# A two-headed state-space kernel on one core: one broadcast load, one first-stage step, one down product and one evacuation change places in a hand-kept order

## The chip, the core and the metric

The kernel runs on one core of a Trainium2 chip. The metric is the time of one execution in device microseconds. TensorE (PE in the profile) multiplies, VectorE (DVE), ScalarE (ACT) and GpSimd (POOL) do the rest, and SyncE (SP) issues nearly all DMAs.

## The reference

Two independent heads, D = 640 channels each, 2048 time steps, bf16 in and out; their outputs stand side by side in the last axis.

```
# head A: diagonal complex state space, P = 640 states
dt = exp(log_dt);  Lam_bar = exp(dt * Lam)
B_bar = ((Lam_bar - 1) / Lam)[:, None] * Bmat
Bu = einsum("bld,pd->blp", x, B_bar)
h[t] = Lam_bar * h[t-1] + Bu[t]            # 2048 steps
y = 2 * Re(einsum("blp,dp->bld", h, Cmat)) + x * Dskip
# head B: gated long convolution
k_shift[t] = sum over j < 4 of k[t-j] * shift_k[j]
kv = k_shift * v
y = irfft(rfft(pad(kv)) * rfft(pad(ssm_k)))[:2048] + kv * ssm_D
out = q * y
```

## The kernel before

Everything lives in one SBUF tile, `arena`, cut into named parts, and one PSUM tile, `acc`, used as eight banks of 512 f32 columns. `build` records 815 operations with their footprints; `depend` derives who must wait for whom. The table `ORDER` then says in which order they are issued, on which engine, and in which bank. An entry `666A6` is operation 666, on ACT (`A`; `V` is DVE, `T` PE, `G` POOL, `S` SP), first bank 6. A small `t` is PE with the product cut into two halves of 64 weight columns ("narrow"), a capital `T` is the full 128-column form, where the operation has both. Each engine executes its own entries strictly in the table's order, and each waits for its operands and for the last reader of its bank. SP is such an engine too: an issue that waits holds back every issue behind it.

Head A turns the recurrence into a tree of 16 time classes. `up2`, `up1` and `up0` multiply x by the scaled B and combine pairs (L581, L602); `coarse` scans 128 blocks (`cs_...`, L679 and the lines near it); `down(n, js)` goes back down the tree in levels 3 to 0: the product `dn` on PE (L229 narrow, L225 full), then the add `ad` on DVE (L728). `project(i)` makes one sixteenth of the output rows: `ld_r` loads x (L736), `xd` multiplies it by D's row (L737), `C` is the product with C (L229 or L225), `ev_C` adds the two (L754), `st_A` stores (L765). D's row is `Dskip` repeated over 128 partitions, 160 KB, loaded once by `ld_Dr` (operation 91, L372); every `xd` reads it, `xd0` first.

Head B does the convolution by Fourier stages as products. `load_h` brings the filter (`ld_h`, L807) and adds `ssm_D` to its first tap (`addD`, L809). `load_kv` brings k and v by transposing DMAs (L814), `conv` makes kv (taps L205 on DVE or L206 on ACT, adds L840, product L841), `plane` writes kv to DRAM (`pl`, L847), and `relay` reads it back in another layout (`rl`, L857). Stage `s1` (L876 full, L881 narrow) is evacuated by `e1` (L886), stage `s2` (L900) by `e2` (L913); the product with the filter is `pp`, `pq`, `py`, `pz` (L924 to L931); `r2` (L951) and `r1` (L972) go back, and `er1`/`em1` multiply by q. Names carry half and unit: `s1h0_5` is first stage, filter, half 0, unit 5; `e2k1_27` evacuates the second stage of kv, half 1, planes 27 to 29.

The operations that the change touches, with their places in the order before:

- `ld_Dr` (91, SP): behind the four `ld_h1` loads of the second half's filter, ahead of `ld_r2`.
- `s1h0_5` (199, PE): behind `up0a_2`, in bank 0; its evacuation `e1h0_5` (200, ACT): behind `e1h0_2` and a small `cf`.
- `dn2_5` (344, PE): narrow, between `dn1_2` and `gC2_1`; its add `ad2_5` follows on DVE.
- `e2k1_27` (666): on ACT, between the evacuations `e2k1_14` and `e2k1_22`.

Of the kernel before, what the change touches and what calls it, by code (L numbers as in the profile page):

```python
# [1097 lines left out]
def plain_order(P):  # L1098
# [16 lines left out]


ORDER = (
# [40 lines left out]
)  # L1158


# [68 lines left out]
```

## Time and profile before

| what | value |
|---|---|
| three runs | 187.65, 188.11, 189.12 us; median 188.11 |
| span of the profiled execution, first to last instruction | 187.3 us |
| PE, DVE, ACT, POOL busy | 175.6, 158.0, 147.7, 72.6 us |
| granted TensorE clock | 0.999 |
| moved by DMA | 30.15 MB, mean 161 GB/s |

The profiler lists no separate time outside its own span for that execution, so the span stands 0.8 us under the median of the runs. A row of the timeline gives the start in microseconds, the duration, the engine, the line and the operation, how many follow each other, and in brackets the idle time of the engine before it with what ended it. A row of the chain gives start, duration and what held the end up then. Engine names with a q are sequencers: an SPq row's duration is the time that SP spent on the issue, not the transfer.

### The profile page before, as it was taken

What the parts mean: (1) busy time and instruction counts of PE and PEld (TensorE: products, weight loads), DVE (VectorE), ACT (ScalarE), POOL (GpSimd) and SP (SyncE); (2) the same over time, 40 slices, a digit from 0 to 9 for tenths busy, and PEclk for the clock granted to TensorE, in tenths of its full rate; (3) what the DMA queues carried; (4) which work ended last, traced back from release to release, by engine and by line L of the source; (5) the groups of instructions that cost most, each with busy time, mean ns of one, the idle gap of its engine ahead of it and who ended that gap; (6) DMA issues with size and microseconds to landing.
All of it is one profiled execution on the core that took longest, in us unless ns stands there. A gap on an engine that the chain in (4) does not pass through costs nothing.

```text
span 187.3 us, 7665 instructions
## 1 busy us (share of the span) xinstructions
PE 175.6 (94%) x3398; PEld 126.3 (67%) x3399; DVE 158.0 (84%) x225; ACT 147.7 (79%) x181; POOL 72.6 (39%) x68
## 2 busy tenths in 40 slices
PE   7998999999799979979997999999999999999992
PEld 2565666677468756656685688776588876887770
DVE  3537964679959899999969999899999999998961
ACT  2469699989899979999997997997898883985000
POOL 8679999900000000008803925730740000551620
PEclk9999999999999999999999999999999999999999
DMA  5999999799999989999989479402496993058996
GB/s 153 191 184 158 200 143 140 141 174 182 198 253 154 290 179 152 180 182 154 138 109 251 154 170 133 75 5 72 122 196 120 210 227 85 15 160 187 208 219 173
DMA packets 106682, 30.15 MB, mean 161 GB/s; under 512 B 101274, under 2 KB 106010, under 8 KB 106650
## 3 DMA queue, kind: packets, MB, share of 16 engines
q1 hardware_dynamic: 106332, 29.35, 86.7%
q8 instruction: 26, 0.43, 1.1%
q10 hardware_dynamic: 318, 0.33, 0.6%
q14 instruction: 6, 0.05, 0.1%
HBM read 11.32 MB, written 7.86 MB: 102 GB/s over the span
## 4 chain that ended last, share of the span: by engine, by line
PE 54%; DVE 23%; DMA 9%; ACT 8%; issue 3%; DVEq 0%; ACTq 0%
PE acc L225 17%; PE acc L581 13%; DMA arena<-in_B_k_dram 9%; PE acc L229 6%; DVE arena L728 6%; PE acc L900 6%; DVE arena L205 5%; ACT arena L913 5%; PE acc L951 4%; DVE arena L840 3%; PE acc L972 3%; PE acc L539 2%; DVE arena L754 2%; PE acc L881 1%; ACT arena L886 1%
## 5 line engine op out<-in xcount | busy, mean ns | idle before, releaser
L581 PE MATMUL acc<-arena 128*64 128x512 bf16 x400 | 45.6, 380 | 1.8 <-DVE arena L457 1.1
L913 ACT CAST arena<-acc 128x960 bf16<-128x960 f32 (+1 forms) x43 | 37.4, 916 | 4.0 <-PE acc L900 2.2
L225 PE MATMUL acc<-arena 128*128 128x320 bf16 (+2 forms) x255 | 36.4, 297 | 2.2 <-DVE arena L754 1.1
L581 PEld LDWEIGHTS <-arena 128*64 128x64 bf16 x400 | 26.0, 110 | 17.8 <-DVE arena L457 1.3
L886 ACT CAST arena<-acc 128x1024 bf16<-128x1024 f32 x37 | 35.8, 1034 | 2.1 <-PE acc L881 2.0
L225 PEld LDWEIGHTS <-arena 128*128 128x128 bf16 x256 | 23.7, 98 | 12.1 <-DVE arena L754 1.3
L841 POOL TENSOR_TENSOR arena<-arena 128x2048 bf16<-128x2048 bf16 x2 | 8.8, 4410 | 53.7 <-DVE arena L840 46.1
L900 PE MATMUL acc<-arena 128*64 128x160 bf16 x512 | 23.6, 235 | 1.8 <-DVE arena L679 1.4
L900 PEld LDWEIGHTS <-arena 128*64 128x64 bf16 x512 | 18.6, 110 | 8.3 <-ACT arena L913 2.2
L229 PE MATMUL acc<-arena 128*64 128x320 bf16 (+3 forms) x258 | 23.2, 313 | 0.5 <-DVE arena L690 0.5
L840 DVE TENSOR_TENSOR arena<-arena 128x2048 bf16<-128x2048 bf16 x14 | 17.6, 1256 | 4.5 <-ACT arena L206 4.3
L728 DVE TENSOR_TENSOR arena<-acc,arena 128x1024 bf16<-128x1024 f32 (+2 forms) x19 | 20.4, 1114 | 0.9 <-PE acc L229 0.5
L760 POOL TENSOR_TENSOR arena<-arena 128x640 bf16<-128x640 f32 x3 | 4.2, 1416 | 32.6 <-ACT arena L752 32.6
L956 ACT CAST arena<-acc 128x1024 bf16<-128x1024 f32 x16 | 15.4, 1025 | 1.7 <-PE acc L951 1.6
L229 PEld LDWEIGHTS <-arena 128*64 128x64 bf16 x258 | 13.0, 110 | 3.5 <-DVE arena L690 0.6
L876 PE MATMUL acc<-arena 128*64 128x128 bf16 x400 | 14.6, 220 | 0.2 <-ACT arena L886 0.2
L876 PEld LDWEIGHTS <-arena 128*64 128x64 bf16 x400 | 12.9, 110 | 2.4 <-ACT arena L886 0.9
L205 DVE TENSOR_SCALAR arena<-arena 128x2048 bf16<-128x2048 bf16 x15 | 11.0, 749 | 3.6 <-DMA arena<-in_B_k_dram 3.5
L754 DVE TENSOR_TENSOR arena<-acc,arena 128x640 bf16<-128x640 f32 x13 | 10.7, 820 | 3.5 <-PE acc L225 2.2
L206 ACT ACTIVATE arena<-arena 128x2048 bf16<-128x2048 bf16 (+2 forms) x10 | 11.1, 1112 | 1.5 <-DMA arena<-in_B_k_dram 1.5
L924 DVE TENSOR_TENSOR arena<-arena 128x2560 bf16<-128x2560 bf16 x8 | 11.9, 1484 | 0.1
L602 PE MATMUL acc<-arena 128*64 128x256 bf16 (+2 forms) x140 | 11.6, 291 | 0.1
(142 smaller groups left out, 284.4 us busy)
## 6 DMA issues: line engine op xcount, KB each, us to landing
out_dram<-arena SPq DMA_DIRECT2D x32, 160.0 KB, 3.3
arena<-in_B_ssm_k_dram SPq DMA_DIRECT2D x8, 320.0 KB, 6.1
kv_rows<-arena SPq DMA_DIRECT2D x5, 512.0 KB, 4.7
arena<-kv_rows SPq DMA_DIRECT2D x16, 160.0 KB, 4.0
arena<-in_A_x_dram SPq DMA_DIRECT2D x16, 160.0 KB, 3.5
arena<-in_B_q_dram SPq DMA_DIRECT2D x8, 320.0 KB, 6.3
arena<-in_A_B_im_dram ACTq DMA_DIRECT2D x1, 160.0 KB, 2.8
arena<-in_A_B_re_dram SPq DMA_DIRECT2D x1, 160.0 KB, 3.0
```

Source lines behind the costliest of these rows:

```text
L205: vm = lambda e: lambda out, in_, by: e.tensor_scalar_mul(out=out, in0=in_, scalar1=by)
L225: e.matmul(out, lhsT=lhsT, rhs=rhs, start=start, stop=stop, skip_group_check=True)
L229: e.matmul(out[half], lhsT=lhsT[:, half], rhs=rhs, start=start, stop=stop, skip_group_check=True, tile_position=(0, 64 * r))
L581: e.matmul(o[64 * r:64 * r + 64], lhsT=self.BT[j][:, r, d, :], rhs=self.XP[:, d, 2 * q:2 * q + 2], start=(d == 0), stop=(d == 4), skip_gro ...
L728: e.tensor_tensor(out=o, in0=b, in1=o, op=ALU.add)
L754: e.tensor_tensor(out=two(ys), in0=two(B)[:, :, 0:320], in1=two(ys), op=ALU.add)
L840: P.add(f"ca{d}_{j}", tt, lambda e: e.tensor_tensor(out=t1, in0=t1, in1=t2, op=ALU.add), outs=[t1], ins=[t1, t2])
L876: e.matmul(B[64 * b:64 * b + 64, 128 * i:128 * i + 128], lhsT=lh[i], rhs=F[:, b, :], start=True, stop=True, tile_position=(0, 64 * b))
L886: P.add(f"e1{what}{hf}_{u}", {PACT: act(1024), PDVE: dve(1024)}, lambda e, B: c.CP[e](out=out, in_=(B.rearrange("p (l n s k) -> p k s l n" ...
L900: e.matmul(B[64 * s:64 * s + 64, 512 * b + 160 * i:512 * b + 160 * i + 160], lhsT=c.W[:, k, 64 * b:64 * b + 64], rhs=self.AS[hf][:, k, 160 ...
L913: c.CP[e](out=out, in_=b.rearrange("p r (k j n) -> p r k j n", k=n, j=4) if nj > 1 else b.rearrange("p r (k x) -> p r k x", k=n))
L956: P.add(f"er2{hf}_{u}", {PACT: act(1024), PDVE: dve(1024)}, lambda e, B: c.CP[e](out=out, in_=B.rearrange("p (s n b) -> p b s n", s=2, n=4 ...
```

## The change

Only the table `ORDER` changes. Its lines are cut anew, so nearly all of them differ as text; as operations, these differ:

```diff
-    "204A0 401S0 140A0 190A4 398V0 199T0 193t2 16A0 138A0 231T4 403V0 194A2 137V0 24V0 402V0 271S0 142A0 200A0 404V0 80A0 197T0 "
+    "386V0 78G0 75A0 262V6 238A0 389S0 79G0 225T2 188V0 254A4 150G0 57A0 201T4 84G0 199T0 200A0 154A0 176S0 195T6 387V0 245T0 196A6 "
...
-    "458V0 439S0 344t4 457V0 351A6 283T0 501T2 345V4 459G0 284A0 348t6 502A2 91S0 466T0 349V6 352t4 467A0 291T2 353V4 470T6 "
+    "442S0 458V0 344T4 351A6 457V0 283T0 501T2 345V4 284A0 459G0 348t6 439S0 502A2 466T0 349V6 352t4 467A0 291T2 353V4 292A2 470T6 "
+    "411S0 301T4 256A6 320V0 410S0 313T0 302A4 316V0 318t2 257T6 447V0 314A0 91S0 415S0 309T4 446V0 258A6 158S0 310A4 319V2 448V0 "
...
-    "641T0 363V6 364t4 753G0 642A0 645T2 365V4 665T6 646A2 376t0 498G0 754S0 666A6 656T2 761S0 377V0 630T4 674S0 657A2 360t6 "
+    "498G0 376t0 754S0 761S0 666V6 377V0 656T2 674S0 630T4 657A2 360t6 675S0 361V6 631A4 632T2 756G0 370t0 633A2 634T4 371V0 652T6 "
```

1. `ld_Dr` is issued ahead of 18 other transfers of SP.
2. `s1h0_5` goes from behind `up0a_2` to between `s1h0_6` and `s1h0_3`, ahead of `s1h0_3`, `up1_4`, `s1h0_1`, `up1_0`, `up21_4`, `s1h0_7`, `s1h0_0` and `up0a_2`; `e1h0_5` goes ahead on ACT from behind `cf` to ahead of `cos`. Both keep bank 0.
3. `dn2_5` is made in the full form: four products of 128 weight columns instead of eight of 64.
4. `e2k1_27` is done by DVE, between the adds `ad0_3` and `ad0_9`, instead of by ACT.

The remaining swaps in the table (`em1` entries on POOL, which issue nothing where DVE did the multiplication, and entries of different engines) leave every engine's instructions as they were.

On SP, at the relay of the first half and at the filter loads of the second (L857 relay, L847 `pl2`, L795 `ld_D`, L736 `ld_r1` and `ld_r2`, L807 `ld_h1`):

```order
 L857 DMA arena<-kv_rows 32x40x64
 L847 DMA kv_rows<-arena 128x2048
+L372 DMA arena<-in_A_Dskip_dram 128x640
 L857 DMA arena<-kv_rows 32x40x64
 L795 DMA arena<-in_B_ssm_D_dram 4x80
...
 L736 DMA arena<-in_A_x_dram 128x640
 L807 DMA arena<-in_B_ssm_k_dram 32x80x64 x4
-L372 DMA arena<-in_A_Dskip_dram 128x640
 L736 DMA arena<-in_A_x_dram 128x640
 L814 DMA_TRANSPOSE arena<-in_B_v_dram 128x2048
```

D's row now stands behind the store `pl2` and ahead of the second relay read; `ld_r2` follows the filter loads directly.

On ACT, in the first stages (L622 `ev_up1_2` and `ev_up1_6`, L314 a table of sines, L478 `cos`, L886 the first-stage evacuations, the upper one of which is `e1h0_5` now and the lower one `e1h0_3`):

```order
 L622 CAST arena<-acc 128x2x2x256 x2
 L314 ACTIVATE arena<-arena 128x1024
+L886 CAST arena<-acc 128x64x2x8
 L478 ACTIVATE arena<-arena 128x1280
 L886 CAST arena<-acc 128x64x2x8
```

One evacuation more stands ahead of `cos`; the same one is missing later, ahead of a table of L354.

On DVE, in the last level of the tree and the second half's second stage (L728 the adds `ad0_2`, `ad0_3`, `ad0_9`, `ad0_1`, `ad0_6`; L913 `e2k1_27`; L924 `pp1`):

```order
 L929 TENSOR_TENSOR arena<-arena 128x8x4x40
 L927 TENSOR_TENSOR arena<-arena 128x8x160
-L728 TENSOR_TENSOR arena<-acc,arena 128x4x256 x5
+L728 TENSOR_TENSOR arena<-acc,arena 128x4x256 x2
+L913 CAST arena<-acc 128x2x3x160
+L728 TENSOR_TENSOR arena<-acc,arena 128x4x256 x3
 L924 TENSOR_TENSOR arena<-arena 128x2560
 L737 TENSOR_TENSOR arena<-arena 128x640
```

The run of five adds is split by one evacuation.

71 rows, old and new, of the table ORDER are left out of this document.

## The prediction

> **What bounds the kernel now.** I first read the page's span, then the busy times of the last part by window, then the chain of waits around the four places that the change touches.
>
> ```profile
> span 187.3 us, 7665 instructions
> 139.00:184.50 45.50, 44.38 (x1064) 34.89 (x1060) 41.01 (x50) 25.84 (x29) 9.79 (x6) 1.00 0.77 162
> ```
>
> The second row is a window: its length, then the busy time of PE, PE's weight loads, DVE, ACT and POOL, the granted clock, the share of the DMA engines and GB/s. From 139 us to the last engine work PE is busy for 44.38 of 45.50 us. So what comes late or early at 139 us comes late or early at the end; nothing in between is left to absorb it.
>
> Before that, who bounds changes by stage. The chain of waits, in two windows (start, duration, what ran or was waited for):
>
> ```profile
> 59.81 5.37 DMA arena<-in_B_k_dram
> ...
> 65.20 1.42 DVE arena L205 x2
> ```
>
> ```profile
> 133.34 1.19 DVE arena L728
> 134.61 1.22 DVE arena L728
> 135.91 1.24 DVE arena L728
> 137.19 1.93 PE acc L900 x48
> ```
>
> From 60 to 67 us the chain is made of a k transfer and what DVE does behind it; PE isn't in it. From 133 to 139 us it goes through three of DVE's five adds, each released by a product and itself releasing a bank, into the products that follow. An instruction given to DVE there is on the path.
>
> Between the two lies the one wait that names D's row:
>
> ```profile
> 95.96 0.53 DVE L809 TENSOR_TENSOR arena<-arena 128x80 bf16<-128x80 bf16 x1
> 97.87 0.49 DVE L737 TENSOR_TENSOR arena<-arena 128x640 bf16<-128x640 bf16 x1 [1.38 <-DMA arena<-in_A_Dskip_dram]
> 98.49 0.82 DVE L754 TENSOR_TENSOR arena<-acc,arena 128x640 bf16<-128x640 f32 x1
> 99.63 1.22 DVE L840 TENSOR_TENSOR arena<-arena 128x2048 bf16<-128x2048 bf16 x1
> 100.77 1.48 DVE L924 TENSOR_TENSOR arena<-arena 128x2560 bf16<-128x2560 bf16 x1
> 102.30 0.82 DVE L754 TENSOR_TENSOR arena<-acc,arena 128x640 bf16<-128x640 f32 x1
> ```
>
> ```profile
> 97.40 1.00 PE L881 MATMUL acc<-arena 64*64 64x64 bf16 x96
> 99.37 2.89 PE L225 MATMUL acc<-arena 128*128 128x320 bf16 x20 [0.97 <-DVE arena L754]
> ```
>
> DVE stands for 1.38 us until the row has landed, then makes `xd0` and `ev_C0`; PE stands for 0.97 us because `C1` needs the bank that `ev_C0` empties.
>
> **Part 1, D's row.** It is gone from its old place. `xd0` can start when `addD1` ends (95.96 + 0.53 = 96.49) and ends near 96.98. `C0`, ahead of the L881 products of 97.40 on PE, ends at about 97.5, so `ev_C0` starts at 97.5 instead of 98.49 and ends at 98.3; `C1` starts when the L881 products leave PE, 98.4 instead of 99.37: 1.0 us. DVE keeps less of it, since the add `ca4_0` (L840, 99.63) needs a tap of ACT:
>
> ```profile
> 96.80 2.04 ACT L206 ACTIVATE arena<-arena 128x2048 bf16<-128x2048 bf16 x1
> ```
>
> The tap ends at 98.84, so the add starts at 98.87, 0.76 earlier, the L924 product ends at 101.48 and `ev_C1` starts at 101.5 instead of 102.30. **0.8 us** stays. I take it to be kept until 133 us, since what follows on PE, DVE and ACT is released by each other's work, which all starts earlier; where it isn't, the last rival holds.
>
> Now the price at the new place, on SP and on the DMA engines:
>
> ```profile
> 64.26 0.42 SPq L857 DMA_DIRECT2D arena<-kv_rows  x1
> 64.74 1.61 SPq L795 DMA_DIRECT2D arena<-in_B_ssm_D_dram  x1
> 67.63 3.23 SPq L857 DMA_DIRECT2D arena<-kv_rows  x4
> 72.74 1.86 SPq L857 DMA_DIRECT2D arena<-kv_rows  x2
> 88.90 1.64 SPq L807 DMA_DIRECT2D arena<-in_B_ssm_k_dram  x1
> 90.58 3.45 SPq L372 DMA_DIRECT2D arena<-in_A_Dskip_dram  x1
> ```
>
> ```profile
> 68.00:95.00 27.00, 25.16 (x586) 17.80 (x583) 26.69 (x35) 26.25 (x33) 8.14 (x2) 1.00 1.08 151
> DMA to landing us min/median/max: 4.8/6.1/7.8
> arena<-kv_rows SPq DMA_DIRECT2D x16, 160.0 KB, 4.0
> ```
>
> The first row is the window from 68 to 95 us; the other two are the times from issue to landing of L807 and, as median, of the relay. An issue of 160 KB takes SP 0.42 us where it needn't queue, and SP's standing from 66.35 (64.74 + 1.61) to 67.63, where it waits for `pl2`, takes that up. The transfer itself isn't free: the DMA engines are full from 68 to 95 us, and 160 KB at 151 GB/s is 1.06 us by which everything behind comes later. Who notices? The last relay read, issued near 73.4, lands near 77.4, then 78.5; its reader starts at 78.65, and PE stands behind it:
>
> ```profile
> 78.65 0.64 PE L876 MATMUL acc<-arena 128*64 128x128 bf16 x16
> 80.09 0.22 PE L225 MATMUL acc<-arena 128*128 128x128 bf16 x1 [0.81 <-ACT arena L886]
> ```
>
> That is 0.15 us of slack and 0.81 us of standing. The last filter load, issued at 88.90, lands near 95.0, at the latest at 95.96, when `addD1` reads it without a wait. With 1.06 more it lands between 96.1 and 97.0; `xd0`, behind it on DVE, then ends between 97.1 and 98.0, and `ev_C0` starts between 97.5 and 98.0. So part 1 gives **−0.8 to −0.4 us**. I take −0.7, nearer to the median landing. The bound on the bad side is the issue's old length, 3.45 us, met again at the new place: that is the second rival, +0.2 us for this part.
>
> **Part 2, the evacuation on DVE.** By form:
>
> ```profile
> L913 ACT CAST arena<-acc 128x960 bf16<-128x960 f32 x33 | 31.1, 978 | 2.0 <-ACT arena L913 0.9 <-PE acc L900 0.3 <-DVE arena L737 0.3
> L913 DVE CAST arena<-acc 128x960 bf16<-128x960 f32 x3 | 3.5, 1154 | 0.0
> ```
>
> ACT loses 0.98 us and DVE gains 1.15 us, between the adds that end at 134.53 (133.34 + 1.19) and start at 134.61. In the chain the adds' steps are 1.30 us for 1.22 to 1.24 us of work: they stand 0.07 to 0.08 us before each for a product. Behind the evacuation the next two products are ready, so these two waits vanish and the cost is 1.15 − 0.15 − 0.08 (instructions of DVE overlap by as much: 100.77 lies before 99.63 + 1.22) = **0.92 us**. The third add of the chain, `ad0_1`, then ends at 138.1 instead of 137.15, the L900 products behind its bank start 0.9 later, and so does `C7` (at 139.12, 137.19 + 1.93), which opens the stretch in which PE is full. ACT has spare time of its own only where PE feeds it late, so its 0.98 us buys nothing. The bounds: 0 if the adds aren't what PE waits for, 1.15 if no wait vanishes; below zero if ACT set the pace there, by its 0.98 us:
>
> ```profile
> 132.71 8.79 ACT L913 CAST arena<-acc 128x960 bf16<-128x960 f32 x11 [0.34 <-PE acc L900]
> ```
>
> ACT runs eleven evacuations without a pause in 8.79 us. I take **+0.9**, since the chain names DVE.
>
> **Part 3, the first-stage step.** It brings a new wait: `up1_4`, behind it on PE, uses bank 0 too.
>
> ```profile
> 37.21 1.09 PE L876 MATMUL acc<-arena 128*64 128x128 bf16 x32
> 38.10 2.35 PE L581 MATMUL acc<-arena 128*64 128x512 bf16 x20
> 40.92 1.01 ACT L622 CAST arena<-acc 128x1024 bf16<-128x1024 f32 x1 [0.62 <-PE acc L602]
> 51.79 1.01 ACT L886 CAST arena<-acc 128x1024 bf16<-128x1024 f32 x1 [0.85 <-PE acc L881]
> 48.12 1.05 PE L581 MATMUL acc<-arena 128*64 128x512 bf16 x8 [1.15 <-DVE arena L457]
> 67.41 0.61 PE L900 MATMUL acc<-arena 128*64 128x160 bf16 x12 [1.39 <-DVE arena L679]
> ```
>
> The first row is `s1h0_6` and `s1h0_3`; `s1h0_5` takes the second's place and ends at 38.3 (37.21 + 1.09). ACT has its evacuation ahead of `cos` now, so it stands until then, and gives the bank free near 39.35 (1.01 us). `up1_4` starts near 39.4 instead of 38.10: 1.3 us late, and queued behind it on PE are `s1h0_1`, `up1_0`, `up21_4`, `s1h0_7`, `s1h0_0` and `up0a_2`. ACT, which begins `cos` only after 39.3, is 2 us late; it gets back its pauses of 0.62 and 0.85 us and the 1.0 us of the evacuation that it no longer makes at 53 us. PE stands 1.15 us before 48.12 for DVE's table, so `up0a_2` is late by 0.2 to 0.4 us, and 1.39 us before 67.41 for DVE, which is behind the k transfer of the chain above. Both engines wait there for something that part 3 doesn't touch. Cost **0** with that cover; up to 1.3 us without it.
>
> **Part 4, the full form of `dn2_5`.**
>
> ```profile
> 87.62 1.49 PE L229 MATMUL acc<-arena 128*64 128x512 bf16 x16
> 89.54 3.48 DVE L728 TENSOR_TENSOR arena<-acc,arena 128x1024 bf16<-128x1024 f32 x3
> ```
>
> Its last product ends at 89.11 and its add starts at 89.54, when DVE comes to it: 0.43 us of slack. The row's 16 products take 1.49 us, eight of them narrow ones of `dn2_5` and these the shorter ones, so the step as a whole is under 0.75 us and a change of its form by 0.43 us isn't to be expected. Cost 0, between −0.1 and +0.1 us. The Trainium skill, TensorEngine Tiling, Key Properties, says that a change of tiling mode drains TensorE, which speaks against one full-width step between `dn1_2`, narrow, and `gC2_1`. By that rule the step's start waits for `dn1_2` to leave the array; the row allows 0.43 us for it, so by the rule too the sum stays unless the drain is longer than that, and no row here times one by itself.
>
> **The sum** is made on the profiled span: 187.3 − 0.7 + 0.9 + 0 + 0 = 187.5 us. The median of the runs stands 0.8 us above the span; with that, **188.3 us**, as good as no change.
>
> **The rivals.**
>
> - *The gain stays, the evacuation is hidden.* ACT's eleven evacuations in a row are the limit from 132 to 141 us, so DVE's time is covered. For it: ACT shows no pause in that stretch. Against it: the chain goes through L728. 188.1 − 0.7 = 187.4 us.
> - *D's row holds up the filter (slower).* SP spends 3.45 us on the issue at 64.7 as it did at 90.58. Of these, 1.28 us vanish in SP's standing until 67.63; 2.2 us reach the filter loads, whose last lands between 97.2 and 98.2. `addD1` and `xd0` follow on DVE, `ev_C0` ends between 99.0 and 100.0 (at 99.31 now), so part 1 turns into −0.3 to +0.7, say +0.2, and part 2 stays. It decides once the last filter load lands later than about 97.4. For it: full DMA engines. Against it: the neighbours' issues of 0.42 us at that very place. 188.1 + 0.2 + 0.9 = 189.2 us.
> - *The first stage doesn't recover.* The 1.3 us at `up1_4` reaches 67 us. For it: ACT and PE are both busy there. Against it: 2.5 us of standing PE in between, and a chain that runs through DMA and DVE. 188.3 + 1.3 = 189.6 us.
> - *The gain doesn't arrive.* Something else ends DVE's wait at the same time, or a later stage is set by something that doesn't start earlier, such as the last v block behind `ld_Dr` on SP and the relay behind that. Then only part 2 is left: 188.1 + 0.9 = 189.0 us. Against it: the wait's own row names D's row, and the last v block, too, is freed of the 1.06 us ahead of it.
>
> **How the numbers follow.** The forecast has a chance of 0.62, the hidden evacuation 0.17, the late filter 0.10, the first stage 0.03, the last 0.05; 0.03 is left for what I don't see. All named cases lie between 187.4 and 189.6 us. With the runs' own spread around them, I take 187.2 to 189.3 us. A measurement of this kernel tells about 1% (1.9 us) from no change. Below 186.2 us none of the cases lies, and above 190.0 us only the first stage together with a late filter; so faster 0.03, same 0.93, slower 0.04.
>
> **What would show it.** Right: no DVE wait that names D's row; `C1` starts within 0.1 us of the L881 products' end; the adds at 133 to 138 us take one evacuation between them, and `C7` starts later relative to `C1` by 0.9 us. PE stands up to 0.9 us near 39 us and ACT 1 us ahead of it, its wait at 48 us nearly vanishes, the rest of the first stage is as before by 67 us. Wrong: a wait of `addD1` for the filter; a wait at L881 near 97 us; a distance from `C1` to `C7` as before (then the evacuation was hidden); a span below 186.5 or above 188.7 us.

## The result and the profile after

The changed kernel takes 189.05 us (median of 19 runs, 188.08 to 190.07), the kernel before 187.79 us on the same chip (19 runs, 187.17 to 191.13). The ratio is 1.0052, interval 1.0033 to 1.0071: 0.98 us slower, 0.62 to 1.33. It is estimated from the runs within 1.5% of the fastest of their kernel, which leaves out one of 191.13 us here and three in the experiment "Row at 29 us" below, and it isn't the quotient of the two medians, which stand 1.26 us apart. The change is under 1%, and the time lies inside the range of 187.2 to 189.3 us; the forecast was 188.3 us, +0.2.

The profiled execution of the changed kernel, its span and its last part by window:

```profile
span 187.9 us, 7657 instructions
139.00:184.50 45.50, 45.10 (x1088) 35.82 (x1082) 41.26 (x51) 26.57 (x30) 9.80 (x6) 1.00 0.76 161
```

This execution took 189.73 us, 1.8 us more than its span, and that distance is the same in the executions profiled later (187.49 for a span of 185.7). By it the profiled execution of before, 187.3 us of span, took 189.1 us: it was the slowest of the three runs shown.

DVE, SP and PE where D's row was awaited:

```profile
94.49 1.23 DVE L840 TENSOR_TENSOR arena<-arena 128x2048 bf16<-128x2048 bf16 x1
97.75 0.53 DVE L809 TENSOR_TENSOR arena<-arena 128x80 bf16<-128x80 bf16 x1 [2.03 <-DMA arena<-in_B_ssm_k_dram]
97.96 0.63 DVE L737 TENSOR_TENSOR arena<-arena 128x640 bf16<-128x640 bf16 x1
98.72 0.82 DVE L754 TENSOR_TENSOR arena<-acc,arena 128x640 bf16<-128x640 f32 x1
```

```profile
63.01 0.42 SPq L372 DMA_DIRECT2D arena<-in_A_Dskip_dram  x1
63.48 1.17 SPq L857 DMA_DIRECT2D arena<-kv_rows  x1
66.15 4.71 SPq L857 DMA_DIRECT2D arena<-kv_rows  x4
78.20 3.80 SPq L814 DMA_TRANSPOSE arena<-in_B_k_dram  x1
84.12 8.74 SPq L807 DMA_DIRECT2D arena<-in_B_ssm_k_dram  x4
```

```profile
98.37 1.00 PE L881 MATMUL acc<-arena 64*64 64x64 bf16 x96 [1.21 <-DVE arena L809]
99.60 2.89 PE L225 MATMUL acc<-arena 128*128 128x320 bf16 x20 [0.23 <-DVE arena L754]
```

The wait for D's row is gone, and a longer one, 2.03 us, stands one instruction earlier: `addD1` waits for the filter. The row's own issue took 0.42 us, as predicted. What grew are the issues behind it: the four relay reads 4.71 us (3.23 before), `ld_k4` 3.80 (2.16 before), the four filter loads 8.74 (7.61 before).

DVE at the five adds, of the kernel before and of the changed one:

```profile
132.18 6.09 DVE L728 TENSOR_TENSOR arena<-acc,arena 128x1024 bf16<-128x1024 f32 x5
138.18 1.48 DVE L924 TENSOR_TENSOR arena<-arena 128x2560 bf16<-128x2560 bf16 x1
```

```profile
132.36 2.36 DVE L728 TENSOR_TENSOR arena<-acc,arena 128x1024 bf16<-128x1024 f32 x2
134.63 1.15 DVE L913 CAST arena<-acc 128x960 bf16<-128x960 f32 x1
135.69 3.48 DVE L728 TENSOR_TENSOR arena<-acc,arena 128x1024 bf16<-128x1024 f32 x3
139.09 1.48 DVE L924 TENSOR_TENSOR arena<-arena 128x2560 bf16<-128x2560 bf16 x1
```

From the first add to the product behind the last, 6.00 us have become 6.73. PE, which had no wait of over 0.15 us in this stretch before, now waits for DVE twice, in the changed kernel:

```profile
135.83 0.62 PE L229 MATMUL acc<-arena 128*64 128x512 bf16 x4 [0.46 <-DVE arena L913]
138.09 1.85 PE L900 MATMUL acc<-arena 128*64 128x160 bf16 x48 [0.23 <-DVE arena L728]
```

The product `C7` starts 40.18 us behind `C1`, which was 39.59: 0.6 us of the 0.73 reach PE.

PE in the first stages:

```profile
37.60 1.53 PE L876 MATMUL acc<-arena 128*64 128x128 bf16 x48
39.84 2.35 PE L581 MATMUL acc<-arena 128*64 128x512 bf16 x20 [0.71 <-ACT arena L886]
42.83 0.64 PE L876 MATMUL acc<-arena 128*64 128x128 bf16 x16 [0.21 <-ACT arena L598]
...
52.71 2.35 PE L581 MATMUL acc<-arena 128*64 128x512 bf16 x20 [0.63 <-ACT arena L886]
...
67.47 1.22 PE L900 MATMUL acc<-arena 128*64 128x160 bf16 x24
...
71.21 0.61 PE L900 MATMUL acc<-arena 128*64 128x160 bf16 x12
```

`up1_4` waits 0.71 us for the new evacuation, and at 52.71 us PE stands again for ACT, 0.63 us, where it had no wait before. In this pair of profiles that seems to cost nothing: PE's waits at 48.12 and 67.41 us are gone and `s2h0_18` starts at 71.21 us, which was 71.54.

So by the two profiles alone the story would be: first stage free, row +0.5, evacuation +0.7. The experiments say that the first of these is false.

### The profile page after: what moved, and what is told of

It reads as the page before. It is cut to its first block, busy times and chain, and to the rows that moved or that the text cites. A ratio compares the mean times of both kernels' runs of the same rounds, so it can differ in the third digit from the quotient of the medians.

```text
span 187.9 us, 7657 instructions
## 1 busy us (share of the span) xinstructions
PE 175.3 (93%) x3395; PEld 123.6 (66%) x3395; DVE 160.4 (85%) x226; ACT 147.3 (78%) x180; POOL 73.4 (39%) x68
## 4 chain that ended last, share of the span: by engine, by line
PE 52%; DVE 17%; ACT 9%; SPq 9%; DMA 8%; issue 3%; DVEq 0%; ACTq 0%
PE acc L581 16%; PE acc L225 14%; PE acc L229 5%; PE acc L900 5%; PE acc L951 5%; DMA arena<-in_B_ssm_k_dram 4%; PE acc L602 4%; SPq L547 4%; DVE arena L728 4%; DMA arena<-in_A_B_im_dram 4%; ACT arena L913 3%; SPq L807 3%; DVE arena L754 2%; ACT arena L886 2%; DVE arena L931 2%
## 5 line engine op out<-in xcount | busy, mean ns | idle before, releaser
L913 ACT CAST arena<-acc 128x960 bf16<-128x960 f32 (+1 forms) x42 | 36.9, 903 | 5.1 <-PE acc L900 3.5
L225 PE MATMUL acc<-arena 128*128 128x320 bf16 (+3 forms) x260 | 37.0, 297 | 1.1 <-DVE arena L684 0.6
L886 ACT CAST arena<-acc 128x1024 bf16<-128x1024 f32 x37 | 35.7, 1033 | 2.7 <-PE acc L881 1.6
L581 PEld LDWEIGHTS <-arena 128*64 128x64 bf16 x400 | 24.4, 110 | 20.0 <-ACT arena L886 1.6
L841 POOL TENSOR_TENSOR arena<-arena 128x2048 bf16<-128x2048 bf16 x2 | 9.3, 4658 | 53.2 <-DVE arena L840 53.2
L900 PE MATMUL acc<-arena 128*64 128x160 bf16 x512 | 23.4, 235 | 0.5 <-DVE arena L728 0.2
L900 PEld LDWEIGHTS <-arena 128*64 128x64 bf16 x512 | 18.7, 110 | 6.6 <-ACT arena L913 1.7
L840 DVE TENSOR_TENSOR arena<-arena 128x2048 bf16<-128x2048 bf16 x14 | 18.5, 1319 | 5.2 <-ACT arena L206 5.0
L728 DVE TENSOR_TENSOR arena<-acc,arena 128x1024 bf16<-128x1024 f32 (+2 forms) x19 | 20.3, 1115 | 0.7 <-PE acc L229 0.5
L229 PEld LDWEIGHTS <-arena 128*64 128x64 bf16 x250 | 12.5, 110 | 4.2 <-DVE arena L728 0.8
L876 PE MATMUL acc<-arena 128*64 128x128 bf16 x400 | 14.4, 220 | 0.4 <-ACT arena L598 0.2
L876 PEld LDWEIGHTS <-arena 128*64 128x64 bf16 x400 | 12.4, 110 | 3.3 <-ACT arena L886 0.9
L754 DVE TENSOR_TENSOR arena<-acc,arena 128x640 bf16<-128x640 f32 x13 | 10.7, 820 | 3.4 <-PE acc L225 2.7
L924 DVE TENSOR_TENSOR arena<-arena 128x2560 bf16<-128x2560 bf16 x8 | 11.9, 1485 | 0.1
L927 DVE TENSOR_TENSOR arena<-arena 128x1280 bf16<-128x1280 bf16 x14 | 11.4, 818 | 0.1
```

The source lines that it names most:

```text
L225: e.matmul(out, lhsT=lhsT, rhs=rhs, start=start, stop=stop, skip_group_check=True)
L229: e.matmul(out[half], lhsT=lhsT[:, half], rhs=rhs, start=start, stop=stop, skip_group_check=True, tile_position=(0, 64 * r))
L581: e.matmul(o[64 * r:64 * r + 64], lhsT=self.BT[j][:, r, d, :], rhs=self.XP[:, d, 2 * q:2 * q + 2], start=(d == 0), stop=(d == 4), skip_gro ...
L728: e.tensor_tensor(out=o, in0=b, in1=o, op=ALU.add)
L754: e.tensor_tensor(out=two(ys), in0=two(B)[:, :, 0:320], in1=two(ys), op=ALU.add)
L840: P.add(f"ca{d}_{j}", tt, lambda e: e.tensor_tensor(out=t1, in0=t1, in1=t2, op=ALU.add), outs=[t1], ins=[t1, t2])
```

## The experiments

Two theories went in. **Theory A**: D's row in front of the filter makes the filter late, and the evacuation is paid; the rest is free. **Theory B**: the late filter belongs to that one execution; the row gains 0.7 us, and the loss is elsewhere. Each run was timed against the kernel before on its own chip. Edits are given as entries of the table; where a kernel starts from the changed one, it says so.

First the table that all of them led to. Every column is a difference of two starts in that kernel's own profile. I: from `s1h0_6` (L876, 37.21 us before) to `s2h0_18` (L900, 71.54). II: from `ca4_1` (L840, 94.79) to `ev_C0` (L754, 98.49). III: from the first of the five adds (L728, 132.18) to `pp1` (L924, 138.18). IV: from the same add to the issue of the store `st_A13`. "k4" is how long SP spent on the issue of `ld_k4`.

| kernel | I | II | III | IV | k4 | ratio to before |
|---|---|---|---|---|---|---|
| before | 34.34 | 3.70 | 6.00 | 52.31 | 2.16 | |
| before, second profile | 32.57 | 4.01 | 6.00 | 52.54 | 2.57 | |
| row alone | 32.22 | 4.15 | 6.00 | 52.79 | 3.57 | 1.0019 (1.0000 to 1.0039) |
| row at 29 us | 33.80 | 2.78 | 6.00 | 52.79 | 2.23 | 1.0008 (0.9975 to 1.0041) |
| evacuation alone | 32.54 | 2.98 | 6.73 | 53.27 | 2.13 | 1.0044 (1.0014 to 1.0075) |
| row, `ld_r1` behind | 32.25 | 2.78 | 6.00 | 52.31 | 2.00 | 1.0030 (1.0001 to 1.0059) |
| `ld_r1` behind | 32.40 | 2.78 | 6.00 | 52.58 | 2.10 | 0.9988 (0.9960 to 1.0017) |
| `ld_r1` behind, `ld_v4` ahead | 32.34 | 3.02 | 6.00 | 52.54 | 2.57 | 0.9992 (0.9965 to 1.0019) |
| change without step | 32.25 | 3.15 | 6.73 | 53.08 | 3.49 | 1.0042 (1.0014 to 1.0069) |
| step and product | 33.61 | 3.40 | 6.00 | 52.31 | 2.28 | 1.0050 (1.0025 to 1.0075) |
| change without row | 33.60 | 3.50 | 6.73 | 52.93 | 2.47 | 1.0072 (1.0047 to 1.0097) |
| change, `ld_r1` behind | 33.61 | 2.91 | 6.73 | 52.94 | 2.27 | 1.0067 (1.0045 to 1.0089) |
| change, second profile | 33.61 | 2.78 | 6.73 | 52.99 | 1.99 | 1.0072 (1.0043 to 1.0101) |
| change | 33.60 | 4.23 | 6.73 | 52.92 | 3.80 | 1.0052 (1.0033 to 1.0071) |

**Row alone.**

```diff
-208A0 415S0 236A4
+208A0 91S0 415S0 236A4
-502A2 91S0 466T0
+502A2 466T0
```

> The kernel before with D's row alone at its new place, ahead of the second relay read. Theory A, the row's bytes and its issue delay everything behind it on SP's full queue, so the last filter load lands at about 97.6 us instead of 95.8 and addD1 waits for it: C1 0.2 to 0.5 us later relative to C0 than before, ratio 1.000 to 1.003. Theory B, the late filter of the profiled execution was an accident and the row by itself does what was predicted: C1 0.7 us earlier, no wait at addD1, ratio 0.995 to 0.998.

Measured: 187.47 us against 186.93, ratio 1.0019. DVE and SP:

```profile
95.37 0.52 DVE L809 TENSOR_TENSOR arena<-arena 128x80 bf16<-128x80 bf16 x1 [1.95 <-DMA arena<-in_B_ssm_k_dram]
```

```profile
76.48 3.57 SPq L814 DMA_TRANSPOSE arena<-in_B_k_dram  x1
82.16 8.33 SPq L807 DMA_DIRECT2D arena<-in_B_ssm_k_dram  x4
```

The same wait and the same long issues as in the changed kernel. The row by itself gains nothing; the interval reaches from 0 to +0.7 us. Theory B's −0.7 us is excluded.

**Change without row.** Against the changed kernel:

```diff
-314A0 91S0 415S0
+314A0 415S0
-468T4 734S0 491A2
+468T4 91S0 734S0 491A2
```

> The changed kernel with D's row back at its old place; the step, the full product and the evacuation on VectorE stay. Theory A: the loss of the row goes and that of the evacuation stays, C1 as in the kernel before, ratio to before 1.002 to 1.004. Theory B: the row's gain of 0.7 us is lost too, ratio 1.007 or more.

Measured: 188.44 us, 1.0072; the intervals of this run and of the changed kernel (1.0052) overlap. That was A's sign but more than A's amount, 1.002 to 1.004, and it is what B asked for. Something beside the evacuation costs.

**Row at 29 us.**

```diff
-55G0 379S0 56G0
+55G0 91S0 379S0 56G0
-502A2 91S0 466T0
+502A2 466T0
```

> The kernel before with D's row alone, put ahead of the transposed load of v near 30 us, where SP stands for 5 us on a wait and the transfer engines are nearly idle, 61 us earlier than before. Theory A, what costs is whose bytes stand ahead of the filter in the full queue: here the row's bytes go into an idle stretch, the filter keeps its time or gains what the row took there, addD1 and xd0 wait for no transfer, C1 0.7 us earlier, ratio 0.995 to 0.997. Rival, any byte added earlier delays the keys' chain and the filter alike because SP's issues follow each other without a gap: C1 as before or later, ratio 1.000 to 1.003. Theory B expects as for the row at its new place, 0.995 to 0.998.

Measured: 188.01 us against 186.93 as medians, ratio 1.0008, interval 0.9975 to 1.0041; its runs spread from 185.60 to 189.62 us. At the place itself A was right: column II is 2.78, `addD1` and `xd0` wait for no transfer. The gain doesn't arrive in the time. In the profiled execution column I is 33.80, and the row's issue took 2.62 us. The stretch wasn't idle: the busy share of the transfer engines from 28 to 32 us is 1.49 to 1.60 in the first profile of the kernel before, more than the 1.08 that the prediction read as full. Not decided whether the earlier bytes made column I long.

**Evacuation alone.**

```diff
-754S0 666A6 656T2
+754S0 666V6 656T2
```

> The kernel before with the evacuation e2k1_27 alone on VectorE between ad0_3 and ad0_9. Theory A, the evacuation is paid for nearly in full by the end: C7 to C13 0.6 to 0.9 us later, ratio 1.003 to 1.005. Rival, it is hidden behind the product that fills the sums' bank: C7 within 0.2 us of before, ratio 0.999 to 1.001. Theory B needs 1.005 or more here, or a loss in the first stage.

Measured: 187.85 us, 1.0044. Column III goes from 6.00 to 6.73, as in every kernel with the edit and in none without. By 139 us it costs 0.73 on DVE; on average over the profiles 0.50 us are left at the last store (column IV: 53.02 over six profiles, 52.52 over eight).

**Step and product.** Only `s1h0_5`, `e1h0_5` and the full `dn2_5` remain. Against the changed kernel:

```diff
-314A0 91S0 415S0
+314A0 415S0
-468T4 734S0 491A2
+468T4 91S0 734S0 491A2
-761S0 666V6 377V0
+761S0 666A6 377V0
```

> The changed kernel with D's row at its old place and the evacuation e2k1_27 back on ScalarE: only the first-stage step and the full down product are left of the change. Theory A: both cost nothing, the stages catch up by 67 us, ratio 0.999 to 1.001. Rival, the late up1_4 keeps 0.3 to 0.6 us of its 1.7 us to the end: ratio 1.002 to 1.003.

Measured: 187.69 us against 186.74, 1.0050, interval 1.0025 to 1.0075. A's 0.999 to 1.001 is excluded; the rival's 1.002 to 1.003 lies at the interval's lower end. PE in this run, then in the second profile of before:

```profile
37.22 1.53 PE L876 MATMUL acc<-arena 128*64 128x128 bf16 x48
39.46 2.35 PE L581 MATMUL acc<-arena 128*64 128x512 bf16 x20 [0.71 <-ACT arena L886]
...
42.46 0.64 PE L876 MATMUL acc<-arena 128*64 128x128 bf16 x16 [0.21 <-ACT arena L598]
...
52.33 2.35 PE L581 MATMUL acc<-arena 128*64 128x512 bf16 x20 [0.63 <-ACT arena L886]
...
67.09 1.22 PE L900 MATMUL acc<-arena 128*64 128x160 bf16 x24
...
70.83 0.60 PE L900 MATMUL acc<-arena 128*64 128x160 bf16 x12
```

```profile
37.35 1.09 PE L876 MATMUL acc<-arena 128*64 128x128 bf16 x32
38.24 2.35 PE L581 MATMUL acc<-arena 128*64 128x512 bf16 x20
...
46.92 2.35 PE L581 MATMUL acc<-arena 128*64 128x512 bf16 x20
...
50.75 2.35 PE L581 MATMUL acc<-arena 128*64 128x512 bf16 x20 [0.22 <-ACT arena L886]
...
65.79 0.61 PE L900 MATMUL acc<-arena 128*64 128x160 bf16 x12 [0.60 <-DVE arena L679]
...
69.92 0.61 PE L900 MATMUL acc<-arena 128*64 128x160 bf16 x12
```

The kernel before has no wait at `up0a_2` here (46.92) and 0.60 us instead of 1.39 at `s2h0_27`. With the step PE has three pauses of over 0.15 us from 37 to 71 us, all for ACT: 0.71, 0.21 and, at 52.33, 0.63 us. The third stands where the kernel before has 0.22: the product waits for the bank that ACT empties by `e1h0_0`. So at `up1_4` the step is 1.35 us late (2.24 us behind `s1h0_6` instead of 0.89), and at this product 1.7 us (15.11 instead of 13.40). Column I is 33.60 or 33.61 in all five profiles with the step. Without it, it is 32.22 to 32.57 in seven profiles and 33.80 and 34.34 in two. The 34.34 is the profile that the prediction read.

**Before, a second profile.** No edit.

> The kernel before, a second profile of it. Theory A: the wait of xd0 for D's row differs between executions, 0.7 to 1.4 us. Theory B: it is 1.4 us again and everything is within 0.3 us of the first profile from 40 us on.

Measured: one execution of 188.73 us, longer than every one of the 29 timed runs of this kernel on its chip (186.11 to 188.12). The wait for the row is 1.25 us, and 0.69 in the kernel with the evacuation alone: A. Theory B's other half is wrong, `s2h0_18` starts 1.62 us earlier than in the first profile.

**Row, and `ld_r1` behind the filter.** The edit of the row alone, and:

```diff
-425T0 729S0 452V0
+425T0 452V0
-478V0 734S0 468T4
+478V0 729S0 734S0 468T4
```

> The kernel before with D's row at its new place and one more transfer of the same 160 KB, ld_r1, moved from ahead of the filter loads to behind them. Theory A, now sharper: the transfer engines are busy without a gap from 20 to 104 us, so the filter lands when the bytes queued ahead of it are through, and the row only took the place of the wait it removed. Then taking ld_r1's bytes from ahead of the filter gives back what the row cost: addD1 waits 1 us less than the 1.95 us of the run with the row alone, C1 1 us earlier than there, ratio 0.996 to 0.998. Rival, the filter waits for its own slow pieces and not for the bytes ahead: wait and ratio as with the row alone, 1.001 to 1.003.

DVE and SP:

```profile
94.77 0.53 DVE L809 TENSOR_TENSOR arena<-arena 128x80 bf16<-128x80 bf16 x1 [0.46 <-DMA arena<-in_B_ssm_k_dram]
94.98 0.63 DVE L737 TENSOR_TENSOR arena<-arena 128x640 bf16<-128x640 bf16 x1
```

```profile
77.14 2.00 SPq L814 DMA_TRANSPOSE arena<-in_B_k_dram  x1
81.03 8.35 SPq L807 DMA_DIRECT2D arena<-in_B_ssm_k_dram  x4
```

In the profile A's wait came out: 0.46 us instead of 1.95, column II 1.37 shorter than with the row alone, and SP reaches the filter loads at 81.03 us instead of 82.16. The Trainium skill, DMA: Bandwidth & Descriptors, "Two DMAs through the same engine are not ordered", says that within one queue of one engine descriptors start in order; this profile agrees, since with one load less ahead of it the filter came earlier, though the second profile of the changed kernel has the filter in time with that load in place. The time did not follow: 187.34 us against 186.74, 1.0030, where 0.996 to 0.998 was expected. The profiled execution, 186.46 us, was the second fastest of the twelve, so its column II needn't be that of the others.

**`ld_r1` behind D's row**, nothing else:

```diff
-425T0 729S0 452V0
+425T0 452V0
-478V0 734S0 468T4
+478V0 729S0 734S0 468T4
```

> The kernel before with ld_r1 alone moved behind D's row, which stays at its old place. Theory A: filter and row land up to 1 us earlier, as far as the filter's issue isn't held by the release of its space at 82.8 us; xd0 no longer waits for the row, xd1 may wait some tenths for ld_r1; C1 0.3 to 0.8 us earlier, ratio 0.996 to 0.999. Rival, the filter's issue is held by its space alone: nothing moves, or xd1 waits for ld_r1 as long as xd0 did for the row, ratio 1.000 to 1.002.

Measured: 186.66 us against 186.74, 0.9988. Column II is 2.78. In the profile 0.3 us were given back between `ev_C0` and the adds (34.09 us, 33.78 in the run above), where GpSimd waited 8.5 us for `ld_v4`, which comes behind row, `ld_r1` and `ld_r2` here; in the run above it waited 6.7.

**The same, with `ld_v4` ahead of `ld_r2`.**

```diff
-425T0 729S0 452V0
+425T0 452V0
-478V0 734S0 468T4 491A2 456S0 499T6
+478V0 729S0 456S0 734S0 468T4 491A2 499T6
```

> The kernel before with ld_r1 behind D's row and ld_v4 ahead of ld_r2: nothing else of the change. Theory A: C0 2.8 to 3.0 us behind ca4_1, cx4 on GpSimd 1 us earlier than with ld_r1 alone moved, the 0.5 us lost there between C1 and C2 back; ratio 0.994 to 0.998, below both kernels. Rival, a transfer moved in a full queue only swaps one wait for another: 0.999 to 1.002.

Measured: 186.62 us against 186.95, 0.9992. GpSimd's wait is 7.4 us and nothing is given back before the adds; DVE:

```profile
94.09 0.53 DVE L809 TENSOR_TENSOR arena<-arena 128x80 bf16<-128x80 bf16 x1 [0.23 <-DMA arena<-in_B_ssm_k_dram]
95.03 0.49 DVE L737 TENSOR_TENSOR arena<-arena 128x640 bf16<-128x640 bf16 x1 [0.40 <-DMA arena<-in_A_Dskip_dram]
```

The expected 0.994 to 0.998 was missed. This and the kernel above are the fastest tried, and neither can be told from the kernel before.

**Change, `ld_r1` behind the filter.** Against the changed kernel:

```diff
-434A6 729S0 452V0
+434A6 452V0
-468T4 734S0 491A2
+468T4 729S0 734S0 491A2
```

> The changed kernel with ld_r1 moved from ahead of the filter loads to behind them. Theory A: the wait of addD1 for the filter, 2.03 us in the changed kernel, falls by about 1.3 us as it did with the row alone; C0 1.3 us nearer to ca4_1 (2.8 us instead of 4.2), ratio to before 0.998 to 1.001, below the changed kernel on the same chip. Rival, the filter's lateness is hidden by what the late first stage costs anyway: ratio as the changed kernel's, 1.004 to 1.007.

Measured: 188.07 us, 1.0067, beside 188.22 for the changed kernel on the same chip. The wait fell to 0.70 us, the time didn't; the rival's ratio came.

**Change without step.** Against the changed kernel:

```diff
-84G0 199T0 200A0 154A0
+84G0 154A0
-398V0 193t2
+398V0 199T0 193t2
-403V0 80A0
+403V0 200A0 80A0
```

> The changed kernel with the first-stage step at its old place; the row, the full product and the evacuation on VectorE stay. Theory A, now with the step as a cost, since the waits of TensorE that were to absorb it belonged to one late execution: s2h0_18 back at 69 to 70 us instead of 70.8 to 71.2, ratio to before 1.002 to 1.006, below the changed kernel's on the same chip. Rival, the loss of the run with step and product came from the full product: no gain from undoing the step, ratio as the changed kernel's or above.

Measured: 187.96 us, 1.0042, beside 1.0072 for the changed kernel; the intervals overlap. Column I is back at 32.25. In this profile 1.1 us went elsewhere: `ca4_1` follows `s2h0_18` by 24.34 us instead of 23.28. SP spent 3.49 us on `ld_k4`; the load of C behind it was issued only at 80.84 us, and PE stood 1.33 us before the product of L571 at 85.76 that reads it. That the load was what it waited for is inferred.

**Change, a second profile.** No edit.

> The changed kernel again, on the chip of the other three. Theory A: s2h0_18 at 70.8 to 71.2 us and the wait of addD1 at 1.9 to 2.1 us as in the first profile of it, ratio to before 1.004 to 1.008. Rival, the late filter was an accident of the first profile: no wait of addD1 above 0.5 us.

Measured: 188.22 us against 186.95, 1.0072. DVE and SP:

```profile
95.19 0.53 DVE L809 TENSOR_TENSOR arena<-arena 128x80 bf16<-128x80 bf16 x1
95.41 0.63 DVE L737 TENSOR_TENSOR arena<-arena 128x640 bf16<-128x640 bf16 x1
96.83 0.82 DVE L754 TENSOR_TENSOR arena<-acc,arena 128x640 bf16<-128x640 f32 x1 [0.79 <-PE acc L229]
```

```profile
77.38 1.99 SPq L814 DMA_TRANSPOSE arena<-in_B_k_dram  x1
82.15 7.45 SPq L807 DMA_DIRECT2D arena<-in_B_ssm_k_dram  x4
```

Here the filter is in time, no wait of `addD1`: the rival of this run. `ev_C0` waits for `C0` on PE, as the prediction had it. `s2h0_18` starts at 70.76 us, just under the 70.8 expected.

## Why the prediction was right, and where it was not

The time was inside the range, near its upper end, but the working behind it did not hold. The gain of the row wasn't there and the step was not free, both to the slow side, against an evacuation that cost less; 0.3 us were given back by the base, since the median before came out at 187.79 us and not 188.11. That the range held was its width and some luck, not the mechanism. Averaged over the profiles of the table:

| term | predicted | measured | from |
|---|---|---|---|
| row | −0.7 | +0.1 to +0.3 | II: 3.58 over four profiles with the row at its new place, 3.52 over five at the old, `ld_r1` unmoved in both; counted from `s2h0_18`, with the 1.1 us lost in "change without step", 27.12 and 26.78 |
| evacuation | +0.9 | +0.7 at `pp1`, +0.5 at the end | III, and the means of IV |
| step | 0 | +0.9 | I: 33.61, mean of the nine without 32.75 |
| product | 0 | 0.03 | `s2h0_18` to `ca4_1`: 23.28 to 23.30 with it, 23.25 or 23.26 without, three profiles with added waits left out (23.44, 23.78, 24.34) |
| sum | +0.2 | +1.5 to +1.7 at the end | timed: +0.98 (0.62 to 1.33) and, with its second profile, +1.35 (0.80 to 1.89) |

Timed one by one, row (+0.35 us), evacuation (+0.82) and step with product (+0.93) add up to +2.1 us, more than the whole change; with intervals of about half a microsecond each, whether they overlap isn't decided.

**Part 3, the step, failed at "Cost 0 with that cover".** The size before the cover was right: 1.3 us late at `up1_4` was forecast and 1.35 came, and column I grew by 1.24 us against the mean of the seven profiles in which PE stands little. The cover was not there. The waits of 1.15 and 1.39 us were those of an execution whose k chain came late: the fourth add of L840 on DVE starts at 42.60 us in it and at 42.38 in the other profile with a long column I (33.80), but at 40.3 to 40.9 in the seven with a short one. In these seven, PE stands 0.60 us at most before `s2h0_27` and nowhere near 48 us; near 50 us it stands 0.18 to 0.22 us for ACT, so that ACT's lateness goes on to PE, as a third pause of 0.63 us. The evacuation that ACT saves in return, `e1h0_5`, stood behind `e1h0_0`, too late to help there. Of the 1.7 us by which PE is then late, 1.0 to 1.4 are left at `s2h0_18`, against the second profile of before (32.57) and the row alone (32.22). Against the recorded execution the step looks free (33.61 and 34.34), which is why the two profiles together hid it; no profile shows the step in an execution with a late k chain. The third rival, "the first stage doesn't recover", with a chance of 0.03, is what mostly happens. Why the k chain is late in some executions stays open.

**Part 1, the row, failed at the landing of the filter.** The prediction let it land between 96.1 and 97.0 us and took the gain of the median. In the changed kernel's first profile `addD1` could start only at 97.75, past the 97.4 us from which the rival of the late filter was to decide; in the second it started at 95.19 without a wait and the gain was there, column II 2.78 against 3.70. Three of the six profiles with the row near 63 us show a wait of `addD1` of 0.9 us or more, and in these three SP stood 3.5 to 3.8 us on `ld_k4`; in the other three, and in all eight without, 2.0 to 2.6. So the rival had the right wait, but not its cause: it looked for a long issue of the row itself, and that took 0.42 us. On average a wait for the row was traded for one for the filter. That the row's bytes delay what is behind them, the prediction's 1.06 us (160 KB are 163,840 bytes, so 1.09), fits the four relay reads: their issues took SP 4.16 to 4.71 us in these six profiles and 3.00 to 3.72 in the eight others. That the bytes ahead of the filter decide is supported by column II, which is 2.78 to 3.02 in the four profiles with `ld_r1` moved behind and 2.78 to 4.23 in the nine with both at either usual place; it isn't settled, since 2.78 came without that move too and the times of those runs show no gain. Why `ld_k4`'s issue has two lengths stays open.

**Part 2, the evacuation, was right in place and sign, and mis-sized.** The term was 1.15 − 0.15 − 0.08 = 0.92. The rows after: evacuation to third add 1.06 (134.63 to 135.69); first add to evacuation 2.27 (132.36 to 134.63), which was 2.43 to the third add (132.18 to 134.61); third add to `pp1` 3.40 (135.69 to 139.09), which was 3.57 (134.61 to 138.18). 1.06 − 0.16 − 0.17 = 0.73: the two waits give back 0.33 instead of the 0.15 predicted, and overlap with the instruction ahead takes 0.09, about as predicted (0.08). The waits were under-read because adds that follow each other without one start 1.13 to 1.14 us apart, less than the 1.19 to 1.24 us that each lasts. A hidden evacuation, the rival with 0.17, is excluded: of the 0.73 us at `pp1`, 0.6 reach `C7` and 0.5 the last store.

**Part 4 was right.** The Trainium skill, TensorEngine Tiling, Key Properties, has a change of mode drain TensorE; on PE the stretch from the L881 product ahead of the step to the L571 product behind it is 1.89 or 1.90 us in the six profiles with the full form and 1.78 or 1.79 in the eight without. So the form and any drain together cost 0.1 us here, within the 0.43 us of slack, and 0.02 to 0.05 us of it are left at `ca4_1`.

**The base.** The sum was made on a span of 187.3 us and set 0.8 us under the median. The distance of time to span is 1.8 us: the recorded span belongs to the run of 189.12 us, 1.0 us above the median on which the sum was set, and its waits were read as if they stood in every run.

Of the signs that were named: the wait for D's row vanished, as said; the wait of `addD1` for the filter and PE's 1.21 us at L881, named as signs of a wrong forecast, came. `C1` started 0.23 us behind the L881 products' end, not within 0.1, and `C7` came 0.6 us later relative to `C1`, not 0.9. PE stood 0.71 and 0.21 us near 40 us, ACT 0.96 us ahead of it, and the wait at 48 us vanished, as said; that looked like proof of Part 3 and was none.

## What to carry to other kernels

A wait counts as cover only if it stands in more than one execution: profile twice before putting a delay into a pause. The length of the profiled run doesn't tell it: both profiled executions of the kernel before were long ones, 189.1 and 188.73 us, and only one of them had the wait of 1.15 us. When a delay goes through two engines, follow it on both: here the second one met PE again 13 us later. In a queue that is never empty, moving one transfer ahead trades waits; ask which transfer then comes last in front of the same reader, and what else in the queue isn't needed before it.

## What the runs showed of the hardware

The issue of one and the same transposing load, `ld_k4`, took SP 2.0 to 2.6 us in eleven profiles and 3.5 to 3.8 us in three, all three with D's row near 63 us ahead of it, as in six profiles in all. Some stretches between two marks, on the other hand, repeat to 0.01 us from execution to execution (column III, on DVE, in fourteen profiles; column I, on PE, in the five with the step). The spread between profiles is larger in column II, 2.78 to 4.23 us, and in column I without the step, 32.22 to 34.34, where a load or what follows one is waited for. One product changed from the 64-column to the 128-column form between narrow neighbours made PE's stretch around it 0.10 to 0.12 us longer, in six profiles against eight.
